# Last 64 rows of two experts: three float32r products on the whole array, or float32 products on two halves of it

## The chip, the cores and the metric

The kernel runs on one core of a Trainium2 chip. The metric is the device time of one execution in microseconds, the median of several; less is better. TensorE is called PE below, VectorE DVE, ScalarE ACT, GpSimd POOL and SyncE SP, as in the profile.

## What is computed

An attention with decay over 8 batches, 8 heads and 576 positions gives 4608 rows of 512 numbers. Each row then goes to one of 8 experts:

```python
logits = x @ w_gate                       # (4608, 512) @ (512, 8)
expert_idx = np.argmax(logits, axis=1)
gate_w = softmax(logits)[rows, expert_idx]
for e in range(8):
    mask = expert_idx == e
    h = np.maximum(x[mask] @ w1[e], 0.0)  # w1[e]: 512 x 1024
    out[mask] = gate_w[mask, None] * (h @ w2[e])   # w2[e]: 1024 x 512
```

All data are float32.

## The kernel before

The first 310 us or so are attention, with the routing of each batch between its steps; then the experts run one after another. Experts 2 to 7 of the program are sorted by their number of rows, so that each has a fixed capacity: `CAPS` is 640 rows for experts 0 to 3, then 608, 576, 576 and 512. Rows that do not fit go through `overflow`, which has no turn here.

An expert e from 1 on has two phases. The "ups" make h: `FT // 2` = 4 rounds of `seven` (L1589), i = 0 to 3, each of 7 products (s = 0 to 6, L1583), a Strassen scheme over two halves of the rows (n = CAPS[e] / 2 columns) and two halves of the weights. A product is 6 matmuls. Every matrix is kept as a high part and a low part (float32r, "hi" and "lo"; hi is rounded on ACT, lo = raw - hi on DVE or POOL), and each block product is hi*hi + lo*hi + hi*lo, three matmuls. In `seven` four PSUM banks a, b, g, d are filled, and ACT and DVE put them together: `A.copy(p1, a)` (L1613 for e = 1, L1616 else) after s = 0, `A.copy(p5, g)` (L1622) after s = 2, `G.tensor_tensor(p5, u3, p5)` on POOL (L1629) after s = 5, and the parts of h that are left over run in the next round as `ends` (L1644): relu to hh on ACT (L1604), h - hh to hl on DVE (L1607). Bank a is written again at s = 4 and bank g at s = 6, with `start=False`: PE must wait there for the two copies. p1, p5, u2 and u3 are one buffer each.

The "downs" (`downs`, L1653) make h @ w2: for each tile m of 128 rows and each quarter q of the 1024 inner numbers one step of 6 matmuls (`down`, L1348): rows of hh or hl as the 128 weights columns, 512 columns of w2 hi or lo moving, into one bank per m (even m in `ps_v`, odd m in `ps_m`). After q = 3 ACT scales the bank by the gate (L1355) and POOL scatters the tile with an indirect DMA (L1380). With 576 rows the last tile, m = 4, has 64 rows: the same 24 matmuls, with 64 weights columns.

w2 of an expert is loaded in four blocks of two inner tiles, `load_v(e, i)` (L1485, 512 KB each, SP's queue), into the tile of the low part; `split_v` rounds it to the tile of the high part (L1499, ACT) and takes the rest in place (L1505, DVE). Blocks 0 and 1 lie in one named tensor of low parts, blocks 2 and 3 in another.

The order on every engine is that of the program, pinned (`order.pin`). Around each step hang tasks by number, in `run` (L1646): in the ups number 7 * i + s, in the downs number 4 * m + q. They load, sum (`sums_s`, L1445 to L1448, POOL) and split w1 of this and the next expert (`split_s`: `round_s` L1460 on ACT, `rest_s` L1466 on DVE or POOL), fetch the next expert's rows (L1172), turn and split them (`turn_t`, `split_t`).

Of the kernel before, what the change touches and what calls it, by code (L numbers as in the profile page):

```python
# [43 lines left out]
SORTED = E - NF  # L44
CAPS = [CAP] * (E - 4) + [608, 576, 576, 512]
# [66 lines left out]
def two_named(c, nc):  # L112
# [16 lines left out]
    for i, (nm, n) in enumerate(sizes):  # L129
# [5 lines left out]
        elif nm == "aT":  # L135
            name(("aT", i - 5), f"aT{i - 5}", n, at)
            for k, (o, values) in enumerate(((0, False), (HW2, True))):
                name(("w2", i - 5, k), f"w2_{i - 5}_{k}", HW2, at + 4 * o, values)
# [959 lines left out]
class Moe:  # L1098
# [127 lines left out]
    def sort_table(self):  # L1226
# [5 lines left out]
        for nm, x in (("gi", gi), ("si", si), ("g", g)):  # L1232
# [16 lines left out]
            mine.append(y)  # L1249
        self.idx["sorted"] = tuple(mine)  # L1250
# [106 lines left out]


# [119 lines left out]
    def w2_part(self, names, i, k):  # L1478

        return names["w2", i // 2, k][:, i % 2 * 2 * D : i % 2 * 2 * D + 2 * D]  # L1480
# [108 lines left out]
    def seven(self, e, i, run, tasks):  # L1589
# [7 lines left out]
        p1, p5, u2, u3 = (self.up_.tile([P, HN], F32, name=f"u{k}")[:, 0:n] for k in range(4))  # L1597
        hh, hl = self.h[e]
# [6 lines left out]

        def rest(src, *at):
            V.scalar_tensor_tensor(place(hl, *at), src, 0.0, place(hh, *at).bitcast(F32),  # L1607
                                   ALU.max, ALU.subtract)

        def after(s):  # L1610
            if s == 0:
                if e == 1:
                    A.copy(p1, a)  # L1613
                self.ends.pop(0)()
                if e > 1:
                    A.copy(p1, a)  # L1616
# [14 lines left out]
        def end():  # L1631
            relu(d, 1, 0)
            relu(p5, 1, 1)
            V.tensor_tensor(g, g, u2, ALU.add)
            rest(d, 1, 0)
# [8 lines left out]
        self.ends = [end, lambda: relu(g, 0, 1), lambda: (rest(p5, 1, 1), rest(g, 0, 1))]  # L1644

    def run(self, run, rest):  # L1646
# [6 lines left out]
        def downs(e, ms, tasks):  # L1653
            k = 0
            for m in ms:
                for q in range(4):
                    run(lambda: self.down(e, m, (2 * q, 2 * q + 2)))
                    for f in tasks.get(k, []):
                        run(f)
                    k += 1  # L1660
# [28 lines left out]
        with tc.tile_pool(name="moe_h", bufs=1) as hp, tc.tile_pool(name="moe_u", bufs=1) as up_, \  # L1689
                tc.tile_pool(name="moe_r", bufs=2) as self.wr:  # L1690
            self.up_ = up_
            hl = hp.tile([P, FT * CAP], F32R, name="hl")
            G = self.nc.gpsimd
            for e in range(1, E):
# [6 lines left out]
                def at(d, *items):  # L1701
# [7 lines left out]
                   (4, S(self.round_s, 2, 1)), (6, S(self.rest_s, 2, 1, G)),  # L1709
                   (late, S(self.load_v, 2)), (late, S(self.load_v, 3)),  # L1710
                   (8, S(self.split_s, 3, 0)), (9, S(self.split_v, 0)),
# [3 lines left out]
                if e == 1:  # L1715
                    at(ups, (0, S(self.sums_s, 3)), (2, S(self.split_s, 2, 0)))
# [15 lines left out]
                else:  # L1732
                    at(ups, (27, lambda: tc.keep_in_program_order(G.drain())))
                    at(ups, (v3, S(self.round_v, 3)))
                    at(dns, (0, S(self.rest_v, 3)), (4, self.count), (8, self.load_count))
                self.ends = [lambda: None] * 3
# [184 lines left out]
```

## Time and profile before

| | us |
|---|---|
| median of 3 runs | 731.15 (729.93 to 731.82) |
| the profiled execution | 730.08 |
| its span, first to last instruction | 728.1 |
| PE busy in it | 718.9 (99%) |
| DVE, ACT, POOL busy | 553.3, 480.2, 434.1 |
| ups of experts 5 and 6 (first row of each to its downs) | 22.1, 22.1 |
| downs of experts 5 and 6 | 29.3, 28.9 |

The page gives each engine's busy time and its share of 40 slices of the span. The trace is then asked for groups of instructions, for waits, and for timelines: instructions in order of time, merged where neighbours have the same line, with the idle time of the engine before them and what ended it in square brackets. The ends of matmuls are modelled and lie some 0.2 us behind the start of the next, so PE's pace is read from the starts.

### The profile page before, as it was taken

The page shows a single profiled execution, that of the slowest core. Times are in us where ns is not written, and L with a number is a line of the kernel's source. Part 1 is how long each engine was busy: PE and PEld are TensorE (multiplying, and loading weights), DVE is VectorE, ACT ScalarE, POOL GpSimd, SP SyncE. Part 2 cuts the span into 40 slices and gives each one's busy share as a digit, 9 for nine tenths or more (in the row PEclk, how much of TensorE's full clock was granted, in tenths as well). Part 3 has the DMA queues.
Part 4 walks back from the last instruction along what each step waited for, and adds up shares of the span by engine and source line. Part 5 has one row for each costly group of instructions (what it writes and reads, how often), then busy time and mean ns, then how long its engine had stood idle before and what let it go on. Part 6 is the DMA issues. An engine that isn't in the chain of part 4 may idle for free. (4 is left out here: it accounts for less than half of the span.)

```text
span 728.1 us, 16528 instructions
## 1 busy us (share of the span) xinstructions
PE 718.9 (99%) x5524; PEld 593.9 (82%) x5524; DVE 553.3 (76%) x1572; ACT 480.2 (66%) x1263; POOL 434.1 (60%) x593
## 2 busy tenths in 40 slices
PE   9999999999999999999999999999999999999996
PEld 6767777777777777889898898898898898898885
DVE  8877989898989899765989478488498498497460
ACT  7899998989898999433666366365365366365431
POOL 6644565656565576835777656566577476576421
PEclk9999999999999999999999999999999999999999
DMA  7988898888888886443383343443433433523301
GB/s 217 251 202 218 217 238 221 230 230 234 219 242 215 225 186 231 146 124 127 102 242 92 139 145 100 135 142 116 144 115 117 167 96 107 174 81 116 134 15 40
DMA packets 82694, 118.16 MB, mean 162 GB/s; under 512 B 9647, under 2 KB 40367, under 8 KB 82608
## 3 DMA queue, kind: packets, MB, share of 16 engines
q1 hardware_dynamic: 75680, 97.18, 48.1%
q0 software_dynamic: 6160, 19.67, 8.1%
q8 instruction: 45, 0.74, 0.4%
q14 instruction: 41, 0.34, 0.2%
q10 hardware_dynamic: 768, 0.25, 0.1%
HBM read 97.88 MB, written 19.63 MB: 161 GB/s over the span
## 5 line engine op out<-in xcount | busy, mean ns | idle before, releaser
L410 ACT ACTIVATE sc<-sc,nmx 128x128 f32<-128x128 f32 (+3 forms) x256 | 143.0, 567 | 2.1 <-DMA wraw<-in_w 1.0
L1583 PE MATMUL ps<-X_0w,w1s 128*128 128x320 f32 (+3 forms) x504 | 105.4, 300 | 0.7 <-ACT u L1622 0.7
L1348 PE MATMUL ps<-w_0w,hhw 128*128 128x512 f32 (+2 forms) x264 | 105.3, 399 | 0.0
L1348 PE MATMUL ps<-w_1w,hhw 128*128 128x512 f32 (+2 forms) x264 | 103.2, 391 | 0.3 <-DVE w_1w L1505 0.3
L1348 PE MATMUL ps<-w_0w,hl 128*128 128x512 f32 (+2 forms) x264 | 103.1, 391 | 0.0
L407 DVE CUSTOM_DVE_ANT_0 sc<-ps,dec 128x384 f32<-128x384 f32 (+2 forms) x192 | 90.2, 506 | 10.6 <-PE ps L423 2.8
L553 PE MATMUL ps<-aT,va_t 128*64 128x256 f32 (+3 forms) x896 | 92.1, 353 | 0.0
L553 PEld LDWEIGHTS ps<-aT,va_t 128*64 128x64 f32 x896 | 57.3, 137 | 31.9 <-issue 6.4
L1583 PEld LDWEIGHTS ps<-X_0w,w1s 128*128 128x128 f32 x504 | 81.7, 188 | 1.5 <-ACT u L1622 1.5
L423 PE MATMUL ps<-raw 64*128 64x256 f32 (+3 forms) x512 | 80.7, 444 | 0.4 <-ACT aT L489 0.4
L1583 PE MATMUL ps<-X_1w,w1s 128*128 128x320 f32 (+3 forms) x252 | 75.3, 299 | 0.0
L1380 POOL DMA_INDIRECT out<-y,so_si x29 | 30.4, 1049 | 72.4 <-ACT y L1355 51.2
L489 ACT COPY aT<-ps 128x512 f32<-128x512 f32 (+4 forms) x154 | 63.0, 453 | 12.5 <-PE ps L493 11.1
L423 PEld LDWEIGHTS ps<-raw 64*128 64x128 f32 x512 | 44.9, 186 | 25.8 <-issue 8.4
L1460 ACT CAST w1s<-w1r 128x1024 fp32r<-128x1024 f32 (+1 forms) x56 | 52.3, 948 | 11.1 <-POOL w1r L1446 10.8
L1466 DVE TENSOR_TENSOR w1s<-w1r,w1s 128x1024 fp32r<-128x1024 f32 (+1 forms) x42 | 52.2, 1257 | 9.2 <-ACT w1s L1460 9.2
L1355 ACT ACTIVATE y<-ps,so_gy 128x512 f32<-128x512 f32 (+2 forms) x28 | 19.3, 690 | 58.9 <-PE ps L1348 42.9
L1348 PEld LDWEIGHTS ps<-w_0w,hl 128*128 128x128 f32 (+2 forms) x264 | 48.5, 184 | 11.8
L1348 PEld LDWEIGHTS ps<-w_1w,hhw 128*128 128x128 f32 (+2 forms) x264 | 48.6, 184 | 10.9 <-DVE w_1w L1505 0.8
L487 DVE COPY aT<-ps 128x384 f32<-128x384 f32 (+4 forms) x118 | 54.2, 493 | 3.6 <-PE ps L493 1.7
L1348 PEld LDWEIGHTS ps<-w_0w,hhw 128*128 128x128 f32 (+2 forms) x264 | 48.5, 184 | 10.2
L1583 PE MATMUL ps<-xa,w1s 128*128 128x320 f32 (+3 forms) x336 | 55.2, 299 | 0.0
(309 smaller groups left out, 1772.9 us busy)
## 6 DMA issues: line engine op xcount, KB each, us to landing
dec<-cd SPq DMA_DIRECT2D x30, 512.0 KB, 5.8
w1r<-in_w SPq DMA_DIRECT2D x112, 128.0 KB, 3.3
w<-in_w SPq DMA_DIRECT2D x28, 512.0 KB, 4.6
raw<-in_qkT SPq DMA_DIRECT2D x63, 160.0 KB, 6.1
raw<-in_qkT SPq DMA_DIRECT2D x64, 144.0 KB, 4.9
decj<-cd SPq DMA_DIRECT2D x30, 288.0 KB, 5.0
va_t<-in_va SPq DMA_DIRECT2D x32, 256.0 KB, 5.7
x_dram<-row SPq DMA_DIRECT2D x32, 256.0 KB, 4.8
```

The source lines that it names most:

```text
L407: V.tensor_tensor_reduce(dst, src, m, -0.125, init, ALU.add, ALU.min, out)
L410: nc.scalar.activation(x, x, AF.Exp, bias=nmx, scale=-1.0, accum_out=acc)
L423: note(nc.tensor.matmul(banks[j][:, o : o + w], r[:, P * t : P * t + P], r[:, QW : QW + w], start=True, stop=n > 1))
L487: V.tensor_copy(dst, src)
L489: nc.scalar.copy(dst, src)
L553: c.last_av = note(nc.tensor.matmul(pv[j * HD : (j + 1) * HD, q0 - qa : qb - qa], l, r, start=(blk == 0), stop=(blk == nb - 1),))
L1348: c.note(nc.tensor.matmul(py, rows(hi_, ft), w[wi], start=(ft + k == 0), stop=(ft == FT - 1 and k == 2),))
L1355: nc.scalar.activation(y[0:n], py, AF.Copy, scale=g[0:n, s : s + 1])
L1380: self.nc.gpsimd.indirect_dma_start(out=self.out, out_offset=bass.IndirectOffsetOnAxis(ap=rows, axis=0), in_=y, in_offset=None, bounds_che ...
L1460: self.nc.scalar.copy(t[:, 0], raw)
L1466: (eng or self.nc.vector).tensor_tensor(lo, raw, hi.bitcast(F32), ALU.subtract)
L1583: self.nc.tensor.matmul(bank, w[:, wi, mat, kt], x[xi][:, kt, :], start=start and k == 0, stop=k == 5, skip_group_check=True,)
```

## The change

The last 64 rows of experts 5 and 6 get float32 products. A new tile `few_rows` holds h of these rows in float32: `keep` copies them there on ACT, twice a round, through relu. `down_few` multiplies them with w2 itself: for each inner tile two products of 64 weights columns by 256 moving columns, the left half of w2 into partitions 0 to 63 of a bank of `ps_s`, the right half into partitions 64 to 127. Two activations scale the halves. The gates are copied to partitions 64 to 127 for it in `sort_table`.

The float32 w2 has to be there again. Blocks 0 to 2 are loaded a second time, over their low parts (`load_v` after steps 9, 11 and 13 of the downs); block 3 is added up from its two parts (`whole_v`, DVE, after step 15). So that these low parts are free in time, the steps of m = 2 and m = 3 alternate by q, and each block of w2 has a name of its own.

In the other experts the space of `few_rows` is a second buffer for p5 in the odd rounds. For e = 1 `A.copy(p1, a)` comes behind the first of the `ends`, as it does for the others, `sums_s(3)` moves from task 0 to 5, `split_s(3, 0)` from 8 to 10 and `split_v(0)` from 9 to 8.

```diff
--- before.py
+++ after.py
@@ -42,6 +42,7 @@
 XM = 2 * (KT // 2) * HN
 NF = 2
 SORTED = E - NF
+FEW = 64
 CAPS = [CAP] * (E - 4) + [608, 576, 576, 512]
 XN = ("T2", "T1", "T4", "T3", "B22")
 
@@ -135,7 +136,9 @@
         elif nm == "aT":
             name(("aT", i - 5), f"aT{i - 5}", n, at)
             for k, (o, values) in enumerate(((0, False), (HW2, True))):
-                name(("w2", i - 5, k), f"w2_{i - 5}_{k}", HW2, at + 4 * o, values)
+                for b in range(2):
+                    name(("w2", 2 * (i - 5) + b, k), f"w2_{2 * (i - 5) + b}_{k}", HW2 // 2,
+                         at + 4 * o + 2 * HW2 * b, values)
             name(("hl", i - 5), f"hl{i - 5}", FT * (CA, CB)[i - 5], at, False)
             for k in range(2 * (i - 5)):
                 name(("w1r", k), f"w1r{k}", 8 * P, at + 4 * (FT * CB + 8 * P * k))
@@ -1247,6 +1250,10 @@
                 V.tensor_copy(u, y)
                 y = u
             mine.append(y)
+        for s in range(n):
+            if CAPS[NF + s] % P == FEW:
+                k = s * NST + CAPS[NF + s] // P
+                V.tensor_copy(mine[2][FEW : 2 * FEW, k : k + 1], mine[2][0:FEW, k : k + 1])
         self.idx["sorted"] = tuple(mine)
 
     def count(self):
@@ -1356,6 +1363,40 @@
         self.scatter(y[0:n], si[0:n, s : s + 1])
 
 
+    def few(self, e):
+
+        if CAPS[e] % P != FEW:
+            return None
+        return self.few_rows
+
+    def down_few(self, e, m, q):
+
+        c, nc = self.c, self.nc
+        _, si, g, s = self.index(e, m)
+        h, n = self.few(e), D // 2
+        if q == 0:
+            self.pf = psum(c.ps_s)
+        w = self.w2_part(c.values, q, 1).rearrange("p (f d) -> p f d", d=D)
+        for f in range(2):
+            for k in range(2):
+                nc.tensor.matmul(self.pf[k * FEW : k * FEW + FEW, 0:n], h[:, 2 * q + f],
+                                 w[:, f, k * n : k * n + n],
+                                 start=q + f == 0, stop=2 * q + f == FT - 1)
+        if q < 3:
+            return
+        y = c.yp.tile([P, D], F32, name="y")
+        for k in range(2):
+            at = slice(k * FEW, k * FEW + FEW)
+            nc.scalar.activation(y[0:FEW, k * n : k * n + n], self.pf[at, 0:n], AF.Copy,
+                                 scale=g[at, s : s + 1])
+        self.scatter(y[0:FEW], si[0:FEW, s : s + 1])
+
+    def whole_v(self, e, i):
+
+        c = self.c
+        hi, lo = (self.w2_part(c.words, i, k).bitcast(F32) for k in range(2))
+        self.nc.vector.tensor_tensor(self.w2_part(c.values, i, 1), hi, lo, ALU.add)
+
     def down_last(self, e, m):
 
         c, nc = self.c, self.nc
@@ -1477,7 +1518,7 @@
 
     def w2_part(self, names, i, k):
 
-        return names["w2", i // 2, k][:, i % 2 * 2 * D : i % 2 * 2 * D + 2 * D]
+        return names["w2", i, k]
 
     def load_v(self, e, i):
 
@@ -1595,6 +1636,8 @@
         n = CAPS[e] // 2
         a, b, g, d = (t[:, 0:n] for t in (a, b, g, d))
         p1, p5, u2, u3 = (self.up_.tile([P, HN], F32, name=f"u{k}")[:, 0:n] for k in range(4))
+        if i % 2 and CAPS[e] % P != FEW:
+            p5 = self.few_rows.rearrange("p f s -> p (f s)")[:, 0:n]
         hh, hl = self.h[e]
 
         def place(h, f, k):
@@ -1602,6 +1645,12 @@
 
         def relu(src, *at):
             A.activation(place(hh, *at), src, AF.Relu)
+
+        few = self.few(e)
+
+        def keep(src, f):
+            if few is not None:
+                A.activation(few[:, f * (FT // 2) + i], src[:, n - FEW : n], AF.Relu)
 
         def rest(src, *at):
             V.scalar_tensor_tensor(place(hl, *at), src, 0.0, place(hh, *at).bitcast(F32),
@@ -1609,11 +1658,8 @@
 
         def after(s):
             if s == 0:
-                if e == 1:
-                    A.copy(p1, a)
                 self.ends.pop(0)()
-                if e > 1:
-                    A.copy(p1, a)
+                A.copy(p1, a)
                 self.ends.pop(0)()
             elif s == 1:
                 V.tensor_tensor(u2, b, p1, ALU.add)
@@ -1631,6 +1677,7 @@
         def end():
             relu(d, 1, 0)
             relu(p5, 1, 1)
+            keep(p5, 1)
             V.tensor_tensor(g, g, u2, ALU.add)
             rest(d, 1, 0)
 
@@ -1641,7 +1688,7 @@
             run(lambda: (self.product(e, i, *args), after(s)))
             for f in tasks.get(7 * i + s, []):
                 run(f)
-        self.ends = [end, lambda: relu(g, 0, 1), lambda: (rest(p5, 1, 1), rest(g, 0, 1))]
+        self.ends = [end, lambda: (relu(g, 0, 1), keep(g, 0)), lambda: (rest(p5, 1, 1), rest(g, 0, 1))]
 
     def run(self, run, rest):
         c, tc = self.c, self.tc
@@ -1652,9 +1699,15 @@
 
         def downs(e, ms, tasks):
             k = 0
-            for m in ms:
-                for q in range(4):
-                    run(lambda: self.down(e, m, (2 * q, 2 * q + 2)))
+            todo = [(m, q) for m in ms for q in range(4)]
+            few = e > 0 and self.few(e) is not None
+            if few:
+                todo[8:16] = [(m, q) for q in range(4) for m in (2, 3)]
+            for m, q in todo:
+                    if few and m == NST - 1:
+                        run(lambda: self.down_few(e, m, q))
+                    else:
+                        run(lambda: self.down(e, m, (2 * q, 2 * q + 2)))
                     for f in tasks.get(k, []):
                         run(f)
                     k += 1
@@ -1690,6 +1743,7 @@
                 tc.tile_pool(name="moe_r", bufs=2) as self.wr:
             self.up_ = up_
             hl = hp.tile([P, FT * CAP], F32R, name="hl")
+            self.few_rows = hp.tile([P, FT, FEW], F32, name="few")
             G = self.nc.gpsimd
             for e in range(1, E):
                 self.h[e] = [t[:, 0 : FT * CAPS[e]].rearrange("p (f s) -> p f s", s=CAPS[e])
@@ -1706,14 +1760,16 @@
                 v2, v3 = (22, 27) if e == 1 or CAPS[e] < CAP else (16, 22)
                 last = G if e == E - 1 else None
                 at(ups, (0, S(self.load_v, 0)), (0, S(self.load_v, 1)),
-                   (4, S(self.round_s, 2, 1)), (6, S(self.rest_s, 2, 1, G)),
+                   (4, S(self.round_s, 2, 1)),
+                       *[(5, S(self.sums_s, 3))] * (e == 1), (6, S(self.rest_s, 2, 1, G)),
                    (late, S(self.load_v, 2)), (late, S(self.load_v, 3)),
-                   (8, S(self.split_s, 3, 0)), (9, S(self.split_v, 0)),
+                   (10 if e == 1 else 8, S(self.split_s, 3, 0)),
+                       (8 if e == 1 else 9, S(self.split_v, 0)),
                    (11, S(self.round_s, 3, 1)), (13, S(self.rest_s, 3, 1, G)),
                    (15, S(self.split_v, 1)), (v2, S(self.split_v, 2, last)),
                    *[(v3, S(self.split_v, 3))] * (e < E - 1))
                 if e == 1:
-                    at(ups, (0, S(self.sums_s, 3)), (2, S(self.split_s, 2, 0)))
+                    at(ups, (2, S(self.split_s, 2, 0)))
                 if e + 1 < E:
                     at(ups, (9, N(self.load_s, 0)), (16, N(self.load_s, 1)),
                        (6, fetch(e + 1, 3)), (6, fetch(e + 1, 4)), (13, fetch(e + 1, 2)),
@@ -1733,6 +1789,9 @@
                     at(ups, (27, lambda: tc.keep_in_program_order(G.drain())))
                     at(ups, (v3, S(self.round_v, 3)))
                     at(dns, (0, S(self.rest_v, 3)), (4, self.count), (8, self.load_count))
+                if self.few(e) is not None:
+                    at(dns, *((9 + 2 * i, S(self.load_v, i)) for i in range(3)),
+                       (15, S(self.whole_v, 3)))
                 self.ends = [lambda: None] * 3
                 for i in range(FT // 2):
                     self.seven(e, i, run, ups)
```

## Rows read from the trace of the kernel before

**Rows 1.** The page: busy time and share of the span.
```profile
PE 718.9 (99%) x5524; PEld 593.9 (82%) x5524; DVE 553.3 (76%) x1572; ACT 480.2 (66%) x1263; POOL 434.1 (60%) x593
```

**Rows 2.** Waits of PE: engine, line, releaser; total us, times, longest.
```profile
PE ps L1583 <- ACT u L1622: 0.7, 3, 0.3
```

**Rows 3.** Timeline of PE, expert 5's tile of 64 rows: start, us, instruction, count.
```profile
621.55 0.40 PE L1348 MATMUL ps<-w_0w,hhw 128*64 128x512 f32 x1
...
627.08 0.69 PE L1583 MATMUL ps<-xa,w1s 128*128 128x288 f32 x4
```

**Rows 4.** Timeline of PE, attention: float32 products on two column halves.
```profile
155.40 1.25 PE L553 MATMUL ps<-aT,va_t 128*64 128x256 f32 x10
...
154.16 2.82 PE L553 MATMUL ps<-aT,va_t 128*64 128x320 f32 x28
...
157.03 0.36 PE L493 MATMUL ps<-identr,sc_Jw 128*128 128x128 f32 x2
```

**Rows 5.** Line L553: its weight loads, ns min/median/max.
```profile
L553 PEld LDWEIGHTS ps<-aT,va_t x896: 132/137/138, 20.7 to 295.2; 128*64 128x64 f32 x180
```

**Rows 6.** Line L1485, w2's loads: time to landing; SP's timeline at expert 5's end.
```profile
DMA to landing us min/median/max: 3.6/4.6/6.0
...
624.28 3.70 SPq L1485 DMA_DIRECT2D w<-in_w  x4
```

**Rows 7.** Timeline of DVE: end of expert 5's downs, and two splits of w2.
```profile
617.23 4.23 DVE L1476 TENSOR_TENSOR X_1w<-X,X_0w 128x576 fp32r<-128x576 f32 x4
628.92 0.46 DVE L1619 TENSOR_TENSOR u<-ps,u 128x288 f32<-128x288 f32 x1 [7.45 <-PE ps L1583]
...
598.57 2.54 DVE L1505 TENSOR_TENSOR w_1w<-w,w_0w 128x1024 fp32r<-128x1024 f32 x1
...
642.41 1.21 DVE L1505 TENSOR_TENSOR w_1w<-w,w_0w 128x1024 fp32r<-128x1024 f32 x1
```

**Rows 8.** Timeline of POOL: two sums of w1 in expert 5's downs.
```profile
622.02 0.74 POOL L1448 TENSOR_TENSOR w1r<-w1r 128x256 f32<-128x256 f32 x1
...
599.92 1.78 POOL L1445 TENSOR_TENSOR w1r<-w1r 128x256 f32<-128x256 f32 x1
```

**Rows 9.** Timeline of PE: three waits before s = 6, experts 1, 1 and 7.
```profile
371.86 0.31 PE L1583 MATMUL ps<-X_1w,w1s 128*128 128x320 f32 x1
372.42 0.57 PE L1583 MATMUL ps<-X_0w,w1s 128*128 128x320 f32 x2 [0.25 <-ACT u L1622]
...
378.54 0.31 PE L1583 MATMUL ps<-X_1w,w1s 128*128 128x320 f32 x1
379.16 0.57 PE L1583 MATMUL ps<-X_0w,w1s 128*128 128x320 f32 x2 [0.31 <-ACT u L1622]
...
692.40 0.28 PE L1583 MATMUL ps<-X_1w,w1s 128*128 128x256 f32 x1
692.86 0.51 PE L1583 MATMUL ps<-X_0w,w1s 128*128 128x256 f32 x2 [0.18 <-ACT u L1622]
```

**Rows 10.** Timeline of ACT, expert 7, round 2: the copy of g.
```profile
692.44 0.37 ACT L1622 COPY u<-ps 128x256 f32<-128x256 f32 x1 [0.27 <-DVE hl L1607]
```

**Rows 11.** Expert 1, rounds 1 and 2: timeline of POOL; PE's s = 4.
```profile
368.81 0.88 POOL L1629 TENSOR_TENSOR u<-u,u 128x320 f32<-128x320 f32 x1
369.65 1.85 POOL L1466 TENSOR_TENSOR w1s<-w1r,w1s 128x768 fp32r<-128x768 f32 x1
...
375.54 0.88 POOL L1629 TENSOR_TENSOR u<-u,u 128x320 f32<-128x320 f32 x1 [1.32 <-DVE u L1627]
...
376.93 1.04 PE L1583 MATMUL ps<-xa,w1s 128*128 128x320 f32 x6
```

**Rows 12.** Expert 6, round 2: ACT's copy of g, and PE's s = 6.
```profile
642.23 0.40 ACT L1622 COPY u<-ps 128x288 f32<-128x288 f32 x1 [0.22 <-DVE hl L1607]
...
642.87 0.42 PE L1583 MATMUL ps<-X_0w,w1s 128*128 128x288 f32 x2
```

**Rows 13.** ACT, groups by shape: the smallest copy of a bank.
```profile
L615 ACT COPY gT<-ps 128x64 f32<-128x64 f32 x8 | 1.7, 218 | 0.0
```

## The prediction

> **What bounds the kernel.** I read the page first: PE is busy for 718.9 of 728.1 us, the other engines for at most three quarters of it [rows 1]. Then PE's own waits: over the whole run the longest group is 0.7 us, three waits for ACT's copy of bank g [rows 2]. So PE's stream sets the end: a microsecond of matmuls taken out is a microsecond of time, and hardly anything is to be had from shorter waits. The question is what the new matmuls cost, and which wait they bring that was covered before.
>
> **The last 64 rows on PE.** Removed are 24 matmuls for each of two experts. In expert 5 they fill 621.55 to 627.08, 5.53 us [rows 3]; expert 6 repeats the pattern. They take 0.23 us each although only half of the array has weights.
>
> Added are 16 float32 products for each expert, 8 pairs of a left and a right half. The attention has this form: 128 inner rows, 64 weights columns, halves in turn. A float32 product leaves two records there: L553 has 896 [rows 5] for 32 head pairs times 14 products. Ten records of 256 columns, five pairs, fill 1.25 us [rows 4]. Ends lie some 0.17 us behind, so a pair takes between (1.25 - 0.17) / 5 = 0.216 and 1.25 / 5 = 0.25 us, and the 16 pairs of records of one expert take 3.46 to 4.0 us. A longer stretch has the switches from and to other matmuls in it: 154.16 to 157.03, 2.87 us [rows 4], is one head pair's whole product, 1600 columns a half, each in two records. The change has 8 * 256 = 2048 columns a half: 2.87 * 2048 / 1600 = 3.67 us. I take this, since both switches are in it. Saved: 5.53 - 3.67 = 1.86 us an expert, 3.7 us in all (3.1 to 4.1).
>
> A weights load of this form takes 0.137 us [rows 5]; two of them, 0.274 us, are longer than the pair's 0.216 to 0.25, so in the attention they run beside each other or beside products. The Trainium skill (TensorEngine Tiling (Array Packing), Restrictions and Gotchas) says that column tiling excludes the fast weight load, which speaks against the change. By loads in single file the sum would be 32 * 0.137 = 4.4 us an expert and the gain 1.1; the attention's pace says otherwise, and I go by that.
>
> **w2 a second time.** Blocks 0 to 2 are loaded again after steps 9, 11 and 13. In the trace SP issues next loads at 624.28, 2.73 us after the tile's start [rows 3, 6]: that is two steps of six matmuls, the end of the last reading of both blocks of a name. So a load goes out at the end of the step that frees it. Block 2 is the tightest: from the end of step 13 PE has steps 14 and 15, at most 5.53 / 4 = 1.38 us each, and steps 16 and 17, 3.67 / 4 = 0.92 us each: 4.6 us. A load lands after 3.6, 4.6 or 6.0 us (least, median, most) [rows 6]. Those went out four in 3.7 us; the new ones leave 2.7 us apart and hardly overlap, so they are nearest to the least. I take 3.6 to 4.4: no wait; the other end is 6.0, a wait of 1.4 us an expert. Blocks 0 and 1 have 8 and 6 us. On SP nothing is queued behind them but the next expert's loads of w2, which cannot go before the tile is done anyway.
>
> Block 3 is summed on DVE after step 15 and needed at step 19, 3 * 0.92 = 2.75 us later. DVE is free: its last split ends at 617.23 + 4.23 = 621.46, as step 16 begins, and then it idles until 628.92 [rows 7]; behind the sum only the next round's work is queued. A sum of this size takes 1.21 us, or 2.54 us when POOL sums too [rows 7, 8]; POOL does so up to 622.76 now. With an estimated 0.25 us to start, it is ready after 1.5 to 2.8 us. I take 1.5 to 2, no wait; the other end is 0.1 us an expert.
>
> The Trainium skill (SBUF — State Buffer, on the shared port pair) says that whichever of the two engines starts first holds the pair for its whole instruction. Then the sum would wait for one POOL sum of 0.74 and end after 2.2 us, in time as well. The rows differ from it: the split of 598.57 was on the way before POOL's sum of 599.92 and was still stretched.
>
> **The order around it.** Steps of m = 2 and 3 alternate: the same matmuls, so nothing on PE. Bank `ps_m` is written again at step 9, one step after m = 1 is done; ACT's scaling of 512 columns takes an estimated 0.7 us, from 0.40 for 288 [rows 12], and a step 5.53 / 4 us [rows 3]: nothing, at most 0.3 us an expert. The scatter of m = 2 comes three steps later on POOL, in front of `sums_s(3)`, and that of m = 3 behind it; what waits for these sums is task 8 of the next ups, over 6 us on: nothing. The two activations instead of one put ACT back by some 0.2 us where it would wait for PE: nothing. The gate copies in `sort_table` are two one-column copies on DVE, long before the first use: nothing.
>
> **ACT's 16 extra copies.** The smallest copy from a bank takes 0.218 us [rows 13]. Two a round come ahead of the copy of g, for which PE waits at s = 6. In expert 6's round 2 that copy ends at 642.63 and s = 6 starts at 642.87 [rows 12]: 0.24 us to spare, and the copy waited 0.22 us for DVE. Two copies, 0.44 us, minus what overlaps: 0 to 0.2 us late in one round of each expert. I take 0; the other end is 0.4 us in all.
>
> **The second p5 buffer and expert 1's order.** The three waits of rows 2 are between 371.86 and 372.42, 378.54 and 379.16, 692.40 and 692.86 [rows 9]. Less a usual distance of 0.15, 0.15 and 0.12 us they cost 0.41, 0.47 and 0.34 us, and some 0.1 us each until the pace is back. In expert 7 the copy waited 0.27 us for DVE's rest of the p5 before [rows 10]; a second buffer takes that wait away: 0.35 us back. The first of expert 1 has the same cause: 0.5 us back. The second doesn't pay. `sums_s(3)`, four sums of 0.74 [rows 8] that ended as the first p5 sum began at 368.81, now run behind that sum, so POOL reaches `rest_s` (369.65) about 1.1 us later. It had 1.32 us idle before the next p5 sum at 375.54 [rows 11], so this comes at about 375.3 and ends at 376.2. Behind it stand ACT's relu and now also the copy of p1, an estimated 0.45 us each for 320 columns, from 0.40 for 288 [rows 12]: 377.1. PE's s = 4, which needs that copy, stood at 376.93 [rows 11] and would now be at 376.4. So a wait of about 0.6 us takes the place of one as long; between 0 and 1.1. Back in all: 0.85 us (0.2 to 1.5).
>
> **Sum.** 3.7 + 0.85 = 4.5 us off the profiled execution's 730.08 gives 725.6. That execution lies 1.1 us under the median of the three runs, so for the median, 731.15, the forecast is 726.6.
>
> **Rivals.** (1) The loads come late. For it: 6.0 us was seen, and the scatter of m = 2 falls into the same time. Against: no second load beside it. At 6.0 us it costs 1.4 us in each expert, and the time is 726.6 + 2.8 = 729.4; at 5.3 us 728.0. It decides from 4.6 us on.
> (2) The rounds pay. ACT's copies cost 0.4, and expert 1's new wait is 1.1 instead of 0.6, with the first wait there left as it is (0.5): 726.6 + 1.4 = 728.0. For it: the 0.24 us of rows 12. Against: ACT waits for DVE at that very place.
> (3) Block 3's sum starts behind POOL and is stretched too, 0.74 us more than the 2.8: 0.8 us an expert, 728.2.
> (4) Slower: the halves don't run side by side in the downs, where both halves take the same weights, while in the attention each half has its own. Then 32 records of 0.216 take 6.9 us and with the switches 7.1, 1.6 us more than now in each expert, and the time is 731.15 + 3.2 - 0.85 = 733.5. It decides from a pair of (5.53 + 0.42) / 16 = 0.37 us on. Against it: five pairs in 1.25 us [rows 4].
>
> **How the numbers follow.** Forecast 0.64, late loads 0.14, rounds 0.10, block 3 0.05, slower 0.05, and 0.02 that nothing changes. A measurement tells 0.3%, 2.2 us, from no change: the line is at 728.96. The late loads lie on either side of it half and half, the rounds at 0.07 to 0.03, block 3 at 0.03 to 0.02. Faster: 0.64 + 0.07 + 0.07 + 0.03 = 0.81; same: 0.07 + 0.03 + 0.02 + 0.02 = 0.14; slower 0.05. The range goes from the best of every term, 4.1 + 1.5 = 5.6 us off, 725.5, less 0.6 for the spread of the runs, 724.9, to the late loads at 6.0 us, 729.4; outside lie the slower case and little else.
>
> **What would show it.** The stretch from the first product of the 64 rows to the next expert's first is 3.7 us instead of 5.53, with pairs every 0.22 us; 7.1 us would be rival 4. A gap before the fifth pair of products, with a DMA as its releaser, is rival 1; one before the seventh, with DVE, rival 3. No wait for the copy of g is left in experts 1 and 7; a wait of s = 4 for the copy of p1 in expert 1's round 2 would show my account of POOL right. New waits before s = 6 in round 2 of experts 5 and 6 are rival 2. The prediction is wrong if PE waits in the new steps for more than 1 us, or if the time off the tile isn't found in the span.

## The result and the profile after

The changed kernel takes 735.36 us (median of six runs) against 731.49 of the kernel before on the same chip: a ratio of 1.0057, 95% interval 1.0038 to 1.0075. One of the six runs took 2821.07 us and is left out of the ratio; the other five lie between 732.78 and 738.42, with a median of 735.05. The forecast was 726.6, range 724.9 to 729.4. It is 8.8 us off, and the kernel got slower where it was to get faster.

Lengths of the stages, each from its first matmul to the next stage's, in the profiled executions (the last column is an experiment below):

| us | before | after | e3_both |
|---|---|---|---|
| profiled execution, span | 730.08, 728.1 | 732.78, 730.9 | 725.62, 723.8 |
| ups of expert 1 | 25.73 | 26.14 | 25.06 |
| downs of experts 5, 6 | 29.32, 28.89 | 27.49, 26.98 | 27.49, 26.98 |
| of them the 64 rows | 5.53 in expert 5 | 3.60, 3.60 | 3.60, 3.60 |
| ups of experts 5, 6, 7 | 22.12, 22.12, 20.54 | 22.12, 25.55, 23.69 | 22.12, 22.22, 20.36 |

The downs gave back what was forecast. The loss is in the ups that come behind them. The page of after, its row of PE (compare rows 1), and PE's waits (compare rows 2):

```profile
PE 715.0 (98%) x5540; PEld 591.5 (81%) x5540; DVE 552.4 (76%) x1576; ACT 481.6 (66%) x1281; POOL 431.8 (59%) x593
```

```profile
PE ps L1624 <- ACT u L1662: 6.7, 5, 2.0
```

PE's busy time fell by 3.9 us, and the span grew. The three small waits for the copy of g [rows 2, 9] are gone. In their place are five for the copy of p1 (L1662), up to 2.0 us each. PE's timeline of after: the tile in expert 5 (compare rows 3), then the three longest waits, in experts 6, 7 and 1, each before s = 4. The other two, 0.62 and 0.93 us, come one round later in experts 6 and 7.

```profile
621.65 3.67 PE L1382 MATMUL ps<-w,few 128*64 128x256 f32 x32
625.25 0.93 PE L1624 MATMUL ps<-xa,w1s 128*128 128x288 f32 x5
...
633.92 0.29 PE L1624 MATMUL pr<-X_1w,w1s 128*128 128x288 f32 x1
636.15 1.06 PE L1624 MATMUL ps<-xa,w1s 128*128 128x288 f32 x6 [1.94 <-ACT u L1662]
...
685.55 0.28 PE L1624 MATMUL pr<-X_1w,w1s 128*128 128x256 f32 x1
687.82 0.38 PE L1624 MATMUL ps<-xa,w1s 128*128 128x256 f32 x1 [2.00 <-ACT u L1662]
...
375.88 0.31 PE L1624 MATMUL ps<-X_1w,w1s 128*128 128x320 f32 x1
377.43 1.15 PE L1624 MATMUL ps<-xa,w1s 128*128 128x320 f32 x6 [1.24 <-ACT u L1662]
```

The tile's 32 records follow each other without a gap, 0.225 us a pair over the tile. So nothing is late in the tile itself. For the wait at 636.15, go back from engine to engine: first ACT, then POOL (compare rows 8).

```profile
625.42 0.95 ACT L1390 ACTIVATE y<-ps,so_gy 64x256 f32<-64x256 f32 x2 [2.93 <-PE ps L1382]
...
631.30 0.41 ACT L1647 ACTIVATE hhw<-ps 128x288 fp32r<-128x288 f32 x1 [0.53 <-DVE ps L1674]
635.22 0.44 ACT L1647 ACTIVATE hhw<-u 128x288 fp32r<-128x288 f32 x1 [3.51 <-POOL u L1675]
635.57 0.24 ACT L1653 ACTIVATE few<-u 128x64 f32<-128x64 f32 x1
635.72 0.38 ACT L1662 COPY u<-ps 128x288 f32<-128x288 f32 x1
```

```profile
621.36 1.00 POOL L1421 DMA_INDIRECT out<-y,so_si  x1 [5.66 <-ACT y L1362]
622.39 0.96 POOL L1486 TENSOR_TENSOR w1r<-w1r 128x256 f32<-128x256 f32 x1
...
625.67 1.00 POOL L1421 DMA_INDIRECT out<-y,so_si  x1 [0.15 <-issue]
633.43 0.93 POOL L1421 DMA_INDIRECT out<-y,so_si  x1 [6.76 <-PE ps L1624]
634.37 0.82 POOL L1675 TENSOR_TENSOR u<-u,u 128x288 f32<-128x288 f32 x1
```

ACT's relu of p5 waits 3.51 us for POOL's sum of p5, and the copy of p1 stands behind that relu. POOL's sum stands behind the scatter of the 64 rows. The rows of that scatter were ready at 626.37, when ACT's two scalings ended (625.42 + 0.95), and it goes out at 633.43. The releaser named there, PE, had long been done. What came at the end is the landing of m = 3's scatter, issued at 625.67 and landed at 632.64, 0.79 us earlier. Scatters write the same tensor, and each waits for the one before it; the trace of before has such a wait by name, 3.73 us before the scatter of 612.24. POOL's rows of before, in the downs of expert 5:

```profile
612.24 1.00 POOL L1380 DMA_INDIRECT out<-y,so_si  x1 [3.73 <-DMA out<-y,so_si]
...
622.92 1.00 POOL L1380 DMA_INDIRECT out<-y,so_si  x1 [0.15 <-issue]
628.28 0.93 POOL L1380 DMA_INDIRECT out<-y,so_si  x1 [4.36 <-ACT y L1355]
```

The time from issue to landing by the scatter's line, first of after, from 615 to 640 (only m = 3's landing is known there), then of before (L1380, from 612 to 640):

```profile
DMA to landing us min/median/max: 7.0/7.0/7.0
```

```profile
DMA to landing us min/median/max: 2.7/3.0/6.5
```

Why did it take 7.0 us? The DMA queues of after, by stretch (packets, MB, share of the 16 engines): first 626 to 629, then 629 to 633.

```profile
q1 hardware_dynamic: 511, 0.99, 99.4%
...
q1 hardware_dynamic: 830, 0.80, 57.9%
q0 software_dynamic: 80, 0.26, 16.7%
```

q0 carries POOL's transfers, and a scatter is 80 packets. Between 626 and 629 none of them moves: SP's queue q1, above all the loads of w2 for the next expert, 2 MB issued from 622.77 on, has the engines for itself. The scatter's packets move after that, while q1's share falls to 57.9%.

### The profile page after: what moved, and what is told of

Same layout as the page of the kernel before. It is cut to its first block, busy times and chain, and to the rows that moved or that the text cites. A ratio compares the mean times of both kernels' runs of the same rounds, so it can differ in the third digit from the quotient of the medians.

```text
span 730.9 us, 16608 instructions
## 1 busy us (share of the span) xinstructions
PE 715.0 (98%) x5540; PEld 591.5 (81%) x5540; DVE 552.4 (76%) x1576; ACT 481.6 (66%) x1281; POOL 431.8 (59%) x593
## 5 line engine op out<-in xcount | busy, mean ns | idle before, releaser
L1355 PE MATMUL ps<-w_0w,hhw 128*128 128x512 f32 (+1 forms) x248 | 99.0, 399 | 0.0
L1355 PE MATMUL ps<-w_0w,hl 128*128 128x512 f32 (+1 forms) x248 | 96.9, 391 | 0.0
L1355 PE MATMUL ps<-w_1w,hhw 128*128 128x512 f32 (+1 forms) x248 | 96.8, 390 | 0.0
L1507 DVE TENSOR_TENSOR w1s<-w1r,w1s 128x1024 fp32r<-128x1024 f32 (+1 forms) x42 | 52.0, 1252 | 9.3 <-ACT w1s L1501 8.1
L1624 PEld LDWEIGHTS ps<-xa,w1s 128*128 128x128 f32 x336 | 48.9, 188 | 9.1 <-ACT u L1662 7.9
L1355 PEld LDWEIGHTS ps<-w_0w,hl 128*128 128x128 f32 (+1 forms) x248 | 46.3, 187 | 10.2
L1665 DVE TENSOR_TENSOR u<-ps,u 128x320 f32<-128x320 f32 (+3 forms) x28 | 13.2, 470 | 54.3 <-PE ps L1624 31.4
L1355 PEld LDWEIGHTS ps<-w_1w,hhw 128*128 128x128 f32 (+1 forms) x248 | 46.4, 187 | 9.1 <-DVE w_1w L1546 0.4
```

Source lines behind the costliest of these rows:

```text
L1355: c.note(nc.tensor.matmul(py, rows(hi_, ft), w[wi], start=(ft + k == 0), stop=(ft == FT - 1 and k == 2),))
L1507: (eng or self.nc.vector).tensor_tensor(lo, raw, hi.bitcast(F32), ALU.subtract)
L1624: self.nc.tensor.matmul(bank, w[:, wi, mat, kt], x[xi][:, kt, :], start=start and k == 0, stop=k == 5, skip_group_check=True,)
L1665: V.tensor_tensor(u2, b, p1, ALU.add)
```

## The experiments

The theory (POOL's queue): the scatter of m = 3 goes out into the next expert's loads, lands late, and the scatter of the 64 rows, waiting for it at the head of POOL's queue, keeps back the sum of p5 and so PE. Rivals: the second loads of w2 are the traffic that hurts; expert 1's new order makes the loss.

**e1_late_scatter.** The scatter of the 64 rows comes at task 7 of the next ups.

```diff
-        self.scatter(y[0:FEW], si[0:FEW, s : s + 1])
+        self.left = lambda: self.scatter(y[0:FEW], si[0:FEW, s : s + 1])
...
+                if self.few(e - 1) is not None:
+                    at(ups, (7, lambda: self.left()))
```

> The changed kernel, with one thing moved: the scatter of the 64 rows is issued on POOL in the next expert's ups at task 7, behind the sum of p5 and the fetches, and not at the end of the tile. Theory (POOL's queue): after the 64 rows this scatter sits at the head of POOL's queue until the scatter before it has landed, and the sum of p5 behind it comes too late for PE's fourth step. Then the ups of experts 6 and 7, 25.5 and 23.7 us in the changed kernel, go to 22.1 to 22.6 and 20.0 to 20.6, and the time lies 2 to 5 us under the kernel before. Rival (ACT: the two scalings and the 16 copies hold up the copy of p1): the ups stay at 25.5 and 23.7 and the time some 3 to 4 us over the kernel before. Rival (the traffic of the second loads holds up data that PE needs): the ups stay long as well, with a DMA or a split as releaser.

Measured: 727.45 us, ratio 0.9959 (0.9947 to 0.9971); ups of experts 6 and 7 at 22.22 and 20.22 us. POOL's timeline:

```profile
625.78 1.00 POOL L1421 DMA_INDIRECT out<-y,so_si  x1 [0.15 <-issue]
631.04 0.80 POOL L1675 TENSOR_TENSOR u<-u,u 128x288 f32<-128x288 f32 x1 [4.25 <-ACT w1s L1501]
...
635.14 1.15 POOL L1421 DMA_INDIRECT out<-y,so_si  x1 [0.31 <-issue]
```

m = 3's scatter goes out at the same time and lands as late, at 633.19. But the sum of p5 no longer stands behind it: 631.04 instead of 634.37. The same loads, and some 7 us gone (the ratios differ by 0.0098; the two stages give 6.8 us): the place in POOL's queue is the cause.

**e4_late_loads.** Meant to put the loads of experts 6 and 7 later by task numbers.

```diff
+                first = 3 if e > 5 else 0
+                late = 5 if e > 5 else late
...
-                at(ups, (0, S(self.load_v, 0)), (0, S(self.load_v, 1)),
+                at(ups, (first, S(self.load_v, 0)), (first, S(self.load_v, 1)),
```

> The changed kernel, with the next expert's four loads of w2 (2 MB) issued some 3 to 4 us later in experts 6 and 7: two at task 3, two at task 5 of the ups. Theory (the scatter of m = 3, which the scatter of the 64 rows waits for, lands late because these loads fill the DMA engines, 7.0 us instead of 2.7): it lands within 3 to 4 us, the sum of p5 is on time, and the ups of experts 6 and 7 go to 22 to 23.3 and 20 to 21.5 us, unless the split of block 0 at task 9 now waits for its load. Rival (the scatter is only issued too late, whatever the traffic): the scatter of the 64 rows still goes out around 633 and the ups stay at 25 us.

Measured: 735.67 us, ratio 1.0072 (1.0048 to 1.0095); ups of experts 6 and 7 at 26.52 and 23.69 us. A miss: SP has nothing ahead of these loads, so it issued them as soon as their space was free, at 624.57 to 627.16, whatever their task. A task number orders work on an engine; it doesn't hold back an engine that has nothing to do. The run repeats the changed kernel and tests neither case of the expectation.

**e6_two_loads_later.** Two of expert 6's four loads stand behind the next load of w1 on SP, which itself has to wait.

```diff
-                late = 9 if e == 1 else 1
+                late = 9 if e == 1 else 10 if e == 6 else 1
...
-                   (late, S(self.load_v, 2)), (late, S(self.load_v, 3)),
+                   *[(late, S(self.load_v, i)) for i in (2, 3) if e != 6],
...
-                    at(ups, (9, N(self.load_s, 0)), (16, N(self.load_s, 1)),
+                    at(ups, (9, N(self.load_s, 0)), *[(late, S(self.load_v, i)) for i in (2, 3) if e == 6],
+                       (16, N(self.load_s, 1)),
```

> The changed kernel, but blocks 2 and 3 of expert 6's w2 are loaded some 10 us later, so that 1 MB and not 2 MB is under way when its ups begin; expert 7's loads are as they were. If the packets of m = 3's scatter stand behind that burst of loads, it lands by about 629 us and not 632.6, the scatter of the 64 rows goes out by 630, and the ups of expert 6 take 22 to 23 us; those of expert 7 stay at 23.7. If the scatter is slow for another reason (its own rows, or its place behind the sums), the ups of expert 6 stay at 25.5.

Measured (one execution, 734.22 us): ups of expert 6 at 23.16 us, of expert 7 at 24.70. POOL and PE (this execution runs some 2.5 us later by then):

```profile
628.23 1.00 POOL L1421 DMA_INDIRECT out<-y,so_si  x1 [0.15 <-issue]
633.54 0.93 POOL L1421 DMA_INDIRECT out<-y,so_si  x1 [4.31 <-ACT w1s L1501]
634.48 0.84 POOL L1675 TENSOR_TENSOR u<-u,u 128x288 f32<-128x288 f32 x1
```

```profile
636.61 0.95 PE L1624 MATMUL ps<-xa,w1s 128*128 128x288 f32 x6
```

The scatter lands after 4.5 us instead of 7.0, and the wait of 1.94 us before s = 4 is gone; 0.54 us is left in round 2. The landing was expected about a microsecond earlier, and the ups come out just over the expected 22 to 23 us. Expert 7, whose loads were not touched, still pays, with a wait of 2.98 us. So the next expert's loads are what delays the scatter, as far as one execution shows it.

**e7_sums_behind.** The sums between the two scatters come behind the second.

```diff
-                       (14, N(self.sums_s, 3)))
+                       (15 if self.few(e) is not None else 14, N(self.sums_s, 3)))
```

> The changed kernel, but the four sums of w1 that stand on POOL between the scatters of m = 2 and m = 3 (sums_s(3) of experts 6 and 7) come one task later, behind m = 3's scatter. If it is enough that this scatter goes out before the loads of the next expert are in full flow, it is issued at about 624 and not 625.7, lands by 629, and the ups of experts 6 and 7 take 22 to 23 and 20.3 to 21.3 us: some 728 us in all. If the scatter stands behind the loads wherever it is issued among them, it still lands at 631 to 632.6, and the ups take 24 to 25.5 and 22 to 23.7 us: 732 to 735 us.

Measured: 734.84 us, ratio 1.0037 (1.0024 to 1.0051); ups of experts 6 and 7 at 26.09 and 24.03 us. POOL:

```profile
624.17 1.00 POOL L1421 DMA_INDIRECT out<-y,so_si  x1 [5.29 <-ACT y L1362]
627.68 0.99 POOL L1421 DMA_INDIRECT out<-y,so_si  x1 [2.51 <-DMA out<-y,so_si]
...
636.77 0.93 POOL L1421 DMA_INDIRECT out<-y,so_si  x1 [5.12 <-PE ps L1624]
```

Without the sums, m = 3's scatter waits 2.51 us for the landing of m = 2's, here by name. It goes out 3.51 us behind it instead of 4.31, still into the loads, and lands after 8.3 us. It is the second case of the expectation, with ups still longer than the 24 to 25.5 and 22 to 23.7 us given there: the sums mostly filled time in which POOL had to wait.

**e5_sum_not_load.** No second loads; all four blocks are added up on DVE.

```diff
-                    at(dns, *((9 + 2 * i, S(self.load_v, i)) for i in range(3)),
-                       (15, S(self.whole_v, 3)))
+                    at(dns, *((9 + 2 * i, S(self.whole_v, i)) for i in range(4)))
```

> The changed kernel, but blocks 0 to 2 of w2 are added up from their two parts on DVE, as block 3 is, and nothing is loaded a second time. If POOL's queue is the cause (the scatter of the 64 rows waits there for the landing of m = 3's, which is late behind the next expert's own loads of w2), the second loads have no part in it: the ups of experts 6 and 7 stay at some 25.5 and 23.7 us, the landing of m = 3's scatter at 7 us, and the time within 0.3% of the changed kernel's, 733 to 737 us. If the second loads are what delays the scatters, the ups go back to 22 and 20.5 us and the time to some 728.

Measured: 737.95 us, ratio 1.0083 (1.0059 to 1.0106). PE's timeline has the tile:

```profile
629.30 1.08 PE L1382 MATMUL ps<-w,few 128*64 128x256 f32 x8 [1.16 <-DVE w L1398]
630.97 1.94 PE L1382 MATMUL ps<-w,few 128*64 128x256 f32 x8 [0.58 <-DVE w L1398]
```

DVE doesn't come through in time. The tiles take 6.65 and 5.43 us, and the ups behind them 22.95 and 22.59. In expert 6 m = 3's scatter, issued at 632.34, lands after 4.8 us instead of 7.0; the next expert's four loads go out over 5.6 us there (627.32 to 632.95), over 2.6 in after. Tile and ups together, 29.60 and 28.02 us, are no better than the 29.15 and 27.29 of after. For the rival the run is inconclusive, since both moved. Two other rows speak against it. In after the second loads were done before m = 3's scatter went out at 625.67: q1 moved no packet between 622.1 and 623.4. And in before, which has no second loads, the scatter of 628.28 landed only at 634.77, after 6.5 us, and nobody waited for it. In these profiles loading again is the cheaper way, by 0.45 and 0.73 us.

**e2_old_order_e1** and **e3_both.** Expert 1's order as before (the second buffer stays); the first is the changed kernel with that alone, the second has e1_late_scatter's edit as well.

```diff
-                       *[(5, S(self.sums_s, 3))] * (e == 1), (6, S(self.rest_s, 2, 1, G)),
+                       (6, S(self.rest_s, 2, 1, G)),
...
-                   (10 if e == 1 else 8, S(self.split_s, 3, 0)),
-                       (8 if e == 1 else 9, S(self.split_v, 0)),
+                   (8, S(self.split_s, 3, 0)), (9, S(self.split_v, 0)),
...
-                    at(ups, (2, S(self.split_s, 2, 0)))
+                    at(ups, (0, S(self.sums_s, 3)), (2, S(self.split_s, 2, 0)))
...
+                if e == 1:
+                    A.copy(p1, a)
                 self.ends.pop(0)()
-                A.copy(p1, a)
+                if e > 1:
+                    A.copy(p1, a)
```

> The changed kernel, with expert 1's tasks and its copy of p1 in the order of the kernel before; the second p5 buffer stays. Theory (the new order costs the wait of 1.5 us before s = 4 in expert 1's round 2, the second buffer alone takes away both old waits before s = 6): expert 1's ups, 25.7 us before and 26.1 in the changed kernel, go to 24.6 to 25.0, and the time goes down by 1.1 to 1.5 us against the changed kernel, still 1.5 to 3 us over the kernel before. Rival (the second buffer itself, or POOL's work, causes the wait): expert 1's ups stay at 26 us. Rival (the old order needs the new one to lose its waits): 25.3 to 25.8 us, with waits before s = 6.

> The changed kernel with both edits: the late scatter of the 64 rows and the old order in expert 1. If POOL's queue and expert 1's order are all that went wrong, PE has 3.7 us less work and hardly a wait more than before: 726 to 727.5 us where the kernel before has 731.5, ratio 0.992 to 0.996. If the time is lost to ACT or to traffic, it stays over the kernel before, at 733 to 734.

Measured: e2 734.25 us, ratio 1.0044 (1.0029 to 1.006); ups of expert 1 at 25.06, of experts 6 and 7 at 26.24 and 25.06 us. e3 725.62 us, ratio 0.9928 (0.9915 to 0.9942): better than both kernels, and no wait before s = 4 left. Both causes are real, and the scatter's is the larger: some 7 us (after against e1). Expert 1's order makes its ups 1.1 us longer (after against e2, e1 against e3). In time it is 2.3 us by the ratios of e1 and e3, whose intervals don't meet; those of after and e2 differ by 1 us, within their intervals.

In e2 the ups of experts 6 and 7 are longer than in after: PE's waits before s = 4 are 2.27 and 3.33 us there. Its stretches around the wait (us, then busy time of PE, PEld, DVE, ACT, POOL, granted clock, DMA share, GB/s), and PE:

```profile
630.00:636.00 6.00, 3.89 (x30) 3.66 (x28) 1.74 (x5) 1.63 (x5) 2.55 (x3) 1.00 0.43 140
636.00:639.40 3.40, 3.24 (x13) 3.24 (x14) 3.26 (x5) 3.40 (x8) 1.99 (x2) 0.50 0.30 70
```

```profile
636.16 1.81 PE L1624 MATMUL ps<-xa,w1s 128*128 128x288 f32 x6 [2.27 <-ACT u L1665]
```

After PE's wait of 2.27 us the granted clock is 0.50, 1.2 GHz, and six matmuls take 1.81 us where after has 1.06. The profiled execution of after, the quickest of its runs, had waits of 1.94 and 2.00 us and kept 2.4 GHz.

**e9_copy_first** and **e10_sums_first.** Which of expert 1's moves costs? Both have the late scatter; the first undoes the place of the copy alone, the second the place of the sums alone (lines of the diff above).

> The changed kernel with the scatter of the 64 rows late (as in e1_late_scatter), and of expert 1's three moves one is undone: the copy of p1 stands ahead of the parts of h that are left over, as before. If expert 1's wait comes of the copy's place behind the relu that needs POOL's sum of p5, it goes, although the sums of w1 and the splits stay where the change put them: ups of expert 1 at 25.0 to 25.4 us instead of 26.1 (28.7 with the slower clock), and 725.5 to 726.5 us. If it comes of POOL's later queue whatever stands behind it, PE still waits 1 us or more at s = 4 or s = 6 and the ups stay at 26.

> The changed kernel with the scatter of the 64 rows late, and of expert 1's three moves another one is undone: the sums of w1 (sums_s(3)) stand at task 0, as before. By the prediction's account, in which these sums put POOL back, the wait before s = 4 goes: ups of expert 1 at 25.1 us and the time at 725.6. If the copy's place alone is enough, the wait stays at 1.2 us and the ups at 26.1, and only the worse case, in which POOL's sum of p5 comes at 376.9 and the clock falls, is gone: 726.5 to 727.5 us.

Measured: e9 727.76 us, ratio 0.9942 (0.9916 to 0.9967), ups of expert 1 at 25.67; e10 726.12 us, ratio 0.9926 (0.9905 to 0.9947), ups at 25.55. Neither account of the expectations holds alone: by the stages of one profile each, either undoing takes about half of the 1.1 us between 26.13 (e1) and 25.06 (e3). The times of e9 and e10 don't tell them apart. In e9 s = 4 starts without a wait, and PE waits 0.25 us for DVE one step later (L1668, at 379.35). In e10 PE still waits at s = 4, but 0.22 us instead of 1.24:

```profile
377.26 1.15 PE L1624 MATMUL ps<-xa,w1s 128*128 128x320 f32 x6 [0.22 <-ACT u L1662]
```

So the long wait takes the copy behind the relu and POOL's late sum together, which is the mechanism of the prediction, and its size was wrong.

**e8_p5_alone.** The kernel before with a second buffer for p5 alone.

```diff
+        if i % 2:
+            p5 = self.few_rows[:, 0:n]
...
+            self.few_rows = hp.tile([P, HN], F32, name="few")
```

> The kernel before with a second buffer for p5 in the odd rounds of all experts, and nothing else of the change. By the prediction's account the waits before s = 6 in experts 1 and 7 that came of the one buffer go: the first of expert 1 gives 0.5 us, that of expert 7 0.35, and, with the sums of w1 where they were, the second of expert 1 too: 0.8 to 1.4 us in all, a ratio of 0.998 to 0.999, the ups of expert 1 at 24.6 to 25.1 us instead of 25.7 and those of expert 7 at 20.1 to 20.3 instead of 20.5. If these waits are only replaced by others, the stages and the time stay as they are.

Measured: 730.85 us, ratio 0.9984 (0.9972 to 0.9996); ups of expert 1 at 25.07 us (25.73 before), of expert 7 at 20.24 (20.54 before). As expected.

## Why the prediction was wrong

**What held.** The downs gave 1.83 and 1.91 us, 3.74 in all; the forecast was 3.7. The tile takes 3.60 us, 3.67 was taken, and rival 4 falls. So do weight loads in single file, which would have made it 4.4 us. The Trainium skill (TensorEngine Tiling (Array Packing), Restrictions and Gotchas) says that column tiling excludes the fast weight load; whether that lengthens the single loads, the trace can't tell: they take 0.137 us in the tile as in the attention. PE waits nowhere in the tile: the second loads and block 3's sum were in time (rivals 1 and 3), the sum at 621.53 for 1.22 us. ACT's copies cost nothing in expert 5's ups, which have them and stay at 22.12 us (the first half of rival 2; its second half, a longer wait in expert 1, came true). The second buffer is worth 0.30 us in expert 7 (e8), against 0.35. In expert 1 it takes away both old waits in e8 and gives 0.66 us, where the prediction put 0.5 on the first alone.

**What failed: the order around the tile.** I followed the scatters of m = 2 and 3 only to the sums of w1 between them, asked who waits for these sums, and wrote "nothing". The scatter of the 64 rows, third in that queue, was not followed. A scatter was counted as an entry in POOL's queue and no more. But the next scatter waits for its landing, and everything behind that waits too, here the sum of p5, the relu, the copy of p1 and PE. The signs were in the trace of before: a scatter that waits 3.73 us for the landing of another stands there by name (612.24), and m = 3's scatter went out at 622.92, ahead of the loads of 624.28 [rows 6], and landed after 2.8 us. The change pushes it to 625.67, behind the first loads. The prediction named a scatter as a danger to the loads (rival 1); the harm went the other way, and none of the signs that I had set down looked at s = 4 of experts 6 and 7; only the last, that the time off the tile must be found in the span, caught it. It costs 25.55 - 22.12 = 3.43 us in expert 6 and, against a forecast of 20.54 - 0.35 = 20.19, 3.50 in expert 7.

**A term of the wrong size: expert 1's new wait.** A wait of 0.6 us (0 to 1.1) was put before s = 4; with 25.73 - 0.5 the ups would be 25.2. They are 26.14, 0.9 more, and from its due time (375.88 + 0.15 = 376.03) to 377.43 PE stood 1.4 us. POOL's sum ended 0.4 us later than I had it, and s = 4 was due 0.4 us earlier than 376.4. The first came of work that stretched on both engines. DVE's split took 2.85 us for 1.21 alone, which put off the operand of the sum (u3, L1673) to 375.47; POOL's fetch of rows (L1175) took 1.79 us where it took 1.04 before, which kept POOL busy until 375.66. I put that down to the new order of the two splits beside the later sums, which the prediction doesn't price; no run undoes the order of the splits alone. In after POOL's rest (L1507) runs first and DVE's split (L1546) beside it:

```profile
370.60 1.85 POOL L1507 TENSOR_TENSOR w1s<-w1r,w1s 128x768 fp32r<-128x768 f32 x1
372.61 1.79 POOL L1175 DMA_INDIRECT xg<-x_dram,so_gi  x1
```

```profile
370.69 2.85 DVE L1546 TENSOR_TENSOR w_1w<-w,w_0w 128x1024 fp32r<-128x1024 f32 x1 [0.95 <-ACT w_0w L1540]
```

In e7_sums_behind ACT's rounding, which waits for the load of w2, came 0.5 us earlier; so did DVE's split, DVE came first, and POOL paid. Its POOL, DVE and PE:

```profile
370.88 2.84 POOL L1507 TENSOR_TENSOR w1s<-w1r,w1s 128x768 fp32r<-128x768 f32 x1
...
376.94 0.86 POOL L1675 TENSOR_TENSOR few<-u,few 128x320 f32<-128x320 f32 x1
```

```profile
370.18 1.82 DVE L1546 TENSOR_TENSOR w_1w<-w,w_0w 128x1024 fp32r<-128x1024 f32 x1 [0.17 <-ACT w_0w L1540]
371.92 2.88 DVE L1507 TENSOR_TENSOR w1s<-w1r,w1s 128x1024 fp32r<-128x1024 f32 x1
```

```profile
378.68 1.77 PE L1624 MATMUL ps<-xa,w1s 128*128 128x320 f32 x6 [2.23 <-ACT u L1662]
```

The wait is then 2.23 us, the clock falls to 1.2 GHz behind it, and expert 1's ups take 28.66 us, 2.5 more than in after's profile. The profiles of e5 and e6 show the same order and the same 28.66; those of e1 and e4 show that of after, and 26.1 to 26.2. Which of the two comes hangs on when the load lands: ACT's rounding waits for it in each of these runs.

**The sum.** The span was to be 728.1 - 4.55 = 723.5 us and is 730.9. Experts 6, 7 and 1 account for 3.43 + 3.50 + 0.91 = 7.8; the rest, -0.4 us, is in small shifts of the start and the last downs. To the median: the profiled execution of after lies 2.3 us under the median of its five runs, 735.05, that of before 1.1. The 1.2 us between them I put down to falls of the clock and to expert 1's worse order: the mean granted clock is 0.998 in the profiled execution of after and 0.992 to 0.996 in the other four. That share is argued, since those executions have no profile. 7.4 + 1.2 = 8.6, and by that median 8.4 were missed; the other 0.3 of the 8.8 comes of the run of 2821.07 us in the median. With the scatter put right and expert 1 in its old order, e3_both's ratio gives 0.9928 * 731.15 = 725.9, within a microsecond of the forecast, though the forecast was for expert 1's new order. The arithmetic of the tile was right, and the order on the helper engines cost nearly twice what the tile gained: 7.1 us between the spans of after and e3, against 3.74.

## What to carry to other kernels

When a step moves on an in-order queue, follow every instruction behind it up to the engine that sets the end, and price a DMA that the next one must wait for by its landing, not by its issue. Look at what else the DMA engines carry when it goes out: the same scatter landed after 2.8 us ahead of a burst of loads and after 7.0 us behind it. A step that frees nothing downstream, like the scatter of a finished tile, belongs behind the work that PE waits for.

## What was not expected of the hardware

**Loads on SP's queue hold up POOL's scatter for 3 us altogether.** q0 moved no packet from 626 to 629 while q1 had 99.4% of the engines. The Trainium skill (DMA: Bandwidth & Descriptors, Queues, rings and completion order) says that each DMA engine takes the queues with work in turn, packet by packet. By that, packets of the scatter that were ready would have moved among the loads'; in the trace of after none moves for these 3 us. Why isn't settled: the trace doesn't show when they were ready, so it neither bears the rule out nor refutes it.

**DVE and POOL take turns by whole instructions.** In after POOL's rest ends at 370.60 + 1.85 = 372.45, and DVE's split, 1.21 us alone [rows 7], ends at 373.54, nearly 372.45 + 1.21. In e7_sums_behind it is DVE first: its split ends at 372.00, and POOL's rest, 1.85 in after, takes 2.84 and ends at 373.72, nearly 372.00 + 1.85. The Trainium skill (SBUF — State Buffer, Who interferes with whom) says that whichever is issued first has the shared ports for its whole instruction and the other blocks. On the whole instruction these rows agree. The prediction read the split of 598.57 as a case to the contrary, by POOL's sum of 599.92. It had left out POOL's instruction before that one:

```profile
599.16 0.82 POOL L1629 TENSOR_TENSOR u<-u,u 128x288 f32<-128x288 f32 x1
```

This ends at 599.98, and the split ends at 601.11, nearly 599.98 + 1.21: turns again. But by its start the split was ahead of it, so who goes first isn't settled by these rows.

**Two levels of PE's clock within one kernel.** The granted clock fell to 0.50 at waits of 2.23 and 2.27 us (e7, e2), and it stayed at 1.00 at those of 1.94 and 2.00 us in after. The length of the wait doesn't decide, though. In e4_late_loads it fell at a wait of 1.98 us in expert 7; in e7_sums_behind it stayed at 1.00 behind a wait of 2.46 us in expert 6. The waits and the stretches behind them, first e4, then e7:

```profile
690.58 1.65 PE L1624 MATMUL ps<-xa,w1s 128*128 128x256 f32 x6 [1.98 <-ACT u L1662]
690.60:693.90 3.30, 3.30 (x15) 3.30 (x16) 3.30 (x5) 3.30 (x6) 0.99 (x1) 0.50 0.02 5
```

```profile
639.48 1.06 PE L1624 MATMUL ps<-xa,w1s 128*128 128x288 f32 x6 [2.46 <-ACT u L1662]
639.50:643.00 3.50, 3.50 (x25) 3.41 (x26) 3.50 (x5) 3.50 (x7) 1.82 (x2) 1.00 0.43 103
```

In e5_sum_not_load it fell behind the two shorter waits in the tile, 1.16 and 0.58 us:

```profile
631.00:634.50 3.50, 3.50 (x15) 2.37 (x16) 0.00 (x0) 0.94 (x2) 2.19 (x3) 0.51 0.82 263
```

So a wait of PE can cost more than its length; by how much isn't to be read from the wait alone.
